# Latent attention and a squared-ReLU layer on one core: value product in 128x32 tiles with a turned result, batch 1's second scores by latents, batch 0's queries in two parts

## The chip, the cores and the metric

One core of one Trainium2 chip runs the whole kernel. The metric is the device time of one launch in microseconds (us), as the median of several runs. Engines: PE (matrix products; its weight loads are listed as PEld), DVE and ACT (elementwise work, copies out of PSUM), POOL (here it issues the loads) and SP (it issues most stores). PSUM has eight banks, numbered 0 to 7 here.

## The reference, cut to what matters

```python
batch, n_heads, seq, head_dim = (8, 8, 576, 64); n_pack = 32
n_tokens, d_model, d_ff = (4608, 512, 2048)

def sm_attn(qq, kk, vv):
    s = scale * np.matmul(qq, kk.transpose(0, 1, 3, 2))
    s = s - np.max(s, axis=-1, keepdims=True)
    a = np.exp(s)
    a = a / (np.sum(a, axis=-1, keepdims=True) + 1e-09)
    return np.matmul(a, vv)
p_packed = sm_attn(p, k, v)            # 32 latents for each head
out = sm_attn(q, p_packed, p_packed)   # 576 tokens look at 32 latents

x = out.transpose(0, 2, 1, 3).reshape(B * S, H * D)
h = x @ w_in
r = np.maximum(h, 0.0)
return (r * r) @ w_out
```

## The kernel before, in words

For each batch, eight heads are worked on as two "quads" (qd) of four. The steps of a batch have names that the plan uses:

- Tk, Tq: DVE turns keys and queries (32x32 blocks) so that the head dimension stands on partitions. `tr_q` turns all 576 positions of a quad at once.
- S1, SX, E: first scores of 32 latents against 576 keys, softmax over the keys, and five 128x128 transposes on PE for each quad, which put the keys on partitions (tile `e1`).
- PV (`pv`, L500 to 511): the value product. The values stand as weights, 128x64, and the softmax weights stream, 32 columns. For each of eight heads five matmuls add up, 40 in a batch. Two column tiles (e = 0, 1) stand beside each other. The result has the head dimension on partitions, which is what the steps behind it want. Quad 0's twenty may be issued before quad 1's softmax is ready.
- XT: `extract` copies that result to `ppT` (bf16), `spread` distributes it over partitions with four small matmuls, and four `pq_block` copies put it into a block-diagonal tile `pq_bd`.
- M (`m`): latents times `w_in`, so that the first layer later needs only the 32 weights a head instead of 64 dimensions. 16 matmuls in a burst, two bursts a batch, each taking a pair of banks and banks 4 and 5.
- S2: second scores. Batches 2 to 7 are in `TURNED`: the latents stand as weights (`s2_both`, L590, 32 matmuls on eight tiles of 64x32), and DVE turns the scores (`s2_turn`, L601) and later the softmax weights (`n_turn`, L609) with 32x32 block transposes. Batch 1 has tokens as weights: `s2` (L578, 16 matmuls), `s2_rest` (L665, 4), and later nine PE transposes (`s2_trh`, L724) with copies. Batch 0 (`SOLO`) does its scores in parts, SA.0.0, SA.0.1, SB.0.1 and SC.0.2, of which the first two need only the first 256 positions.
- C, N: softmax over 32 latents, and its result with latents on partitions (`a2`).
- F1: first layer, ReLU and square (for batch 0 in two parts: FA on 256 tokens, F1 on 320); 16 blocks of 128 features a batch. F2: second layer for each of 36 tiles of 128 tokens, 16 matmuls of 512 columns each, in the order of the feature blocks fb = 0 to 15; block fb needs pair fb // 2 of `w_out`, loaded as b0 to b7.

Nothing of the order is fixed by the source. A planner (`Plan`, L54 to 245) runs when the program is built: every step has pieces with an engine and a booked duration, what it depends on, which PSUM banks it takes and when it frees them; a list scheduler puts the ready piece of lowest priority number on its engine, and the instructions are issued in the order that comes out. A step's priority is a level plus a number from `TABLE` (L248 to 293). For a load it is -200 + 5 x (its place in `ORDER`) plus that number:

```python
ORDER = ("k0 v0 q0 i0 a0 a1 a2 a3 b0 b1 k1 b2 b3 v1 b4 b5 q1 b6 b7 p2 "
         + " ".join(f"k{b} v{b} q{b}" for b in range(2, B)))
```

Here a is `w_in`, b is `w_out`. The loads up to k2 are streams of their own, so their priorities alone set their order on POOL; those behind come in the order of the list. All are issued by POOL. In front of the output matmuls, where PE would be idle, the planner puts matmuls on zeros (`keep_clock`, L348), whose results nobody reads. Matmuls of different tile shapes belong to different modes, and the planner books 0.098 us for each change of mode (`TURN`).

Of the kernel before, what the change touches and what calls it, by code (L numbers as in the profile page):

```python
# [8 lines left out]
ACT = mybir.ActivationFunctionType  # L9
ALU = mybir.AluOpType  # L10
AX = mybir.AxisListType
F32 = mybir.dt.float32
# [41 lines left out]
class Plan:  # L54
# [193 lines left out]
TABLE = {'o': {'P.0': -451.53, 'X.0': -384.22, 'P.2': -273.87, 'X.1': -102.86, 'La0': -820.75, 'La1': -800.82,  # L248
# [45 lines left out]


def kernel_impl(tc, q, k, v, p, w_in, w_out, out):
    nc = tc.nc
    B, H, S, Dh = q.shape
    assert Dh == D and S == JT * 32 and H == 2 * QH
    NQD = H // QH  # L300
    DMODEL, DFF = w_in.shape
    NE = w_out.shape[1]
    NFB = DFF // FB
# [14 lines left out]
    with ExitStack() as ctx:  # L318
# [36 lines left out]
        def bank(u, j=0):  # L355
            return half(u[j])
# [827 lines left out]
```

## Time and profile before

| | us |
|---|---|
| median of 3 runs | 252.06 (251.58 to 252.1) |
| the profiled execution, time | 252.03 |
| the profiled execution, span | 250.3 |
| PE busy in the span | 239.2 |
| DVE busy | 185.2 |
| ACT busy | 165.7 |
| granted PE clock, mean | 0.999 |

Times in the views are counted from the start of the span. A timeline row gives start, duration, engine, line, operation, output and input tiles, form and count; in square brackets stands how long the engine was idle ahead of it and what ended that. A matmul's duration includes its way through the array, so what a burst costs PE is read from its first start to the first start behind it. Rows of groups give total busy time, then the mean in nanoseconds of one instruction. Rows of windows give the stretch, its length, and the busy time of PE, PEld, DVE, ACT and POOL with counts. Copies out of PSUM have the lines of a helper (L364 on ACT, L366 on DVE), so they are told apart by their tiles.

### The profile page before, as it was taken

How to read it: one execution, taken by the hardware profiler on the slowest of the kernel's cores; microseconds unless marked ns; L12 is line 12 of the kernel's file. 1: busy time of each engine (PE TensorE's matmuls, PEld its weight loads, DVE VectorE, ACT ScalarE, POOL GpSimd, SP SyncE). 2: the span in 40 equal slices, each digit the busy share in tenths (PEclk: the TensorE clock that was granted, in tenths of full speed). 3: DMA queues.
4: the chain of work that ended last, by engine and by line, in shares of the span. 5: the costliest groups of instructions: out<-in, count | busy, mean ns of one | idle time of the engine just before them, and what ended most of it. 6: DMA issues, size and time to landing. Idle time of an engine off the chain costs nothing.

```text
span 250.3 us, 5864 instructions
## 1 busy us (share of the span) xinstructions
PE 239.2 (96%) x2334; PEld 133.2 (53%) x2334; DVE 185.2 (74%) x356; ACT 165.7 (66%) x292; POOL 43.0 (17%) x76
## 2 busy tenths in 40 slices
PE   6788999999999999999999999999999999999992
PEld 4464465365544665466453564565435554466641
DVE  5779868794799999847698899646998667866100
ACT  8548799587638668699457688588066853587010
POOL 8845553423343310000000000000000000000000
PEclk9999999999999999999999999999999999999999
DMA  6999999999999999611111110310222102301222
GB/s 105 200 204 207 202 197 208 204 242 242 204 224 243 206 245 195 137 50 45 42 45 38 50 42 3 87 43 0 66 64 59 27 3 63 101 6 42 76 77 61
DMA packets 26715, 28.50 MB, mean 114 GB/s; under 512 B 5440, under 2 KB 18112, under 8 KB 26688
## 3 DMA queue, kind: packets, MB, share of 16 engines
q0 software_dynamic: 18960, 18.55, 45.2%
q1 hardware_dynamic: 6960, 9.32, 13.6%
q8 instruction: 18, 0.29, 0.4%
q10 hardware_dynamic: 768, 0.26, 0.4%
q14 instruction: 9, 0.07, 0.1%
HBM read 37.22 MB, written 9.44 MB: 186 GB/s over the span
## 4 chain that ended last, share of the span: by engine, by line
PE 80%; DMA 16%; issue 1%; POOL 1%; ACT 1%; DVE 0%; ACTq 0%; DVEq 0%; POOLq 0%
PE pb L806 46%; PE ps L750 22%; DMA w_out_b<-in_moe_w_out_dram 9%; DMA v_b<-in_v_dram 7%; PE ps L564 2%; PE pb L509 2%; PE ps L469 2%; PE pb L823 1%; PE pb L494 1%; PE pb L564 1%; PE ps L597 1%; PE pb L597 0%; POOL k_b L414 0%; ACT pq_bd L364 0%; PE pb L521 0%
## 5 line engine op out<-in xcount | busy, mean ns | idle before, releaser
L806 PE MATMUL pb<-w_out_b,gT 128*128 128x512 bf16 x560 | 144.0, 380 | 0.8 <-ACT gT L779 0.5
L806 PEld LDWEIGHTS <-gT 128*128 128x128 bf16 x560 | 51.8, 98 | 56.5 <-issue 6.0
L788 ACT ACTIVATE r<-ps 128x576 bf16<-128x576 f32 x112 | 71.0, 652 | 15.0 <-PE ps L750 11.6
L750 PE MATMUL ps<-a,M 128*128 128x288 bf16 x448 | 70.9, 286 | 0.0
L798 DVE TENSOR_TENSOR gT<-r 128x576 bf16<-128x576 bf16 x112 | 49.2, 453 | 26.3 <-ACT r L788 25.7
L750 PEld LDWEIGHTS <-M 128*128 128x128 bf16 x448 | 43.4, 98 | 22.3 <-issue 2.3
L364 ACT COPY o_sb<-pb 128x512 f32<-128x512 f32 (+1 forms) x17 | 9.6, 568 | 25.2 <-PE pb L806 21.2
L366 DVE COPY o_sb<-pb 128x512 f32<-128x512 f32 (+2 forms) x21 | 13.4, 641 | 14.7 <-PE pb L823 12.8
L481 ACT ACTIVATE e1x<-ps,n 128x576 bf16<-128x576 f32 x16 | 11.8, 738 | 13.1 <-DVE n L477 11.9
L364 ACT CAST M<-ps 128x1024 bf16<-128x1024 f32 (+1 forms) x15 | 14.7, 982 | 3.6 <-PE ps L564 3.6
L364 ACT CAST M<-pb 128x512 bf16<-128x512 f32 x28 | 15.5, 598 | 0.0
L709 ACT ACTIVATE e<-d 128x1152 bf16<-128x1152 f32 (+2 forms) x9 | 9.1, 1010 | 7.7 <-DVE d L704 7.6
L477 DVE TENSOR_REDUCE n<-ps 128x1 f32<-128x576 f32 x16 | 11.6, 749 | 3.2 <-PE ps L469 2.8
L419 POOL DMA_DIRECT2D v_b<-in_v_dram x16 | 11.2, 699 | 13.6 <-DMA k_b<-in_k_dram 4.6
L445 DVE STREAM_TRANSPOSE kT<-k_b 128x576 f32<-128x576 f32 x16 | 11.8, 756 | 2.0 <-DMA k_b<-in_k_dram 2.0
L414 POOL DMA_DIRECT2D q_b<-in_q_dram x16 | 8.9, 561 | 22.9 <-DVE kT L445 11.6
L442 DVE STREAM_TRANSPOSE qT<-q_b 128x576 f32<-128x576 f32 x16 | 11.8, 758 | 0.8 <-DMA q_b<-in_q_dram 0.7
L715 DVE TENSOR_REDUCE t<-e 128x36 f32<-128x1152 bf16 (+2 forms) x9 | 10.3, 1150 | 2.5 <-ACT e L709 2.4
L350 PE MATMUL pb<-zero 128*128 128x256 bf16 x64 | 10.4, 307 | 1.1 <-DVE zero L369 1.1
L364 ACT COPY e<-pb 128x640 bf16<-128x640 bf16 x14 | 9.5, 699 | 2.8 <-PE pb L494 2.8
L414 POOL DMA_DIRECT2D k_b<-in_k_dram x16 | 8.7, 544 | 13.9 <-DMA q_b<-in_q_dram 4.1
L721 DVE TENSOR_TENSOR n<-e,r 128x1152 bf16<-128x1152 bf16 (+2 forms) x9 | 10.4, 1157 | 0.2
(95 smaller groups left out, 232.9 us busy)
## 6 DMA issues: line engine op xcount, KB each, us to landing
out_dram<-o_sb SPq DMA_DIRECT2D x141, 64.0 KB, 1.7
k_b<-in_k_dram POOLq DMA_DIRECT2D x16, 288.0 KB, 12.0
q_b<-in_q_dram POOLq DMA_DIRECT2D x16, 288.0 KB, 12.0
v_b<-in_v_dram POOLq DMA_DIRECT2D x8, 320.0 KB, 12.2
v_b<-in_v_dram POOLq DMA_DIRECT2D x8, 256.0 KB, 11.8
w_in_b<-in_moe_w_in_dram POOLq DMA_DIRECT2D x8, 256.0 KB, 10.1
w_out_b<-in_moe_w_out_dram POOLq DMA_DIRECT2D x8, 256.0 KB, 10.6
p_b<-in_p_dram POOLq DMA_DIRECT2D x1, 192.0 KB, 10.6
```

What stands on the lines that cost most here:

```text
L364: nc.scalar.copy(dst, src)
L366: eng.tensor_copy(dst, src)
L414: nc.gpsimd.dma_start(t, src[self.b, qd * QH:(qd + 1) * QH].rearrange("h (a j) d -> (h a) (j d)", j=JT))
L419: nc.gpsimd.dma_start(self.v[64 * i:64 * i + 64, :, :n * D], src[:, :, i * GM * D:(i * GM + n) * D])
L442: nc.vector.transpose(self.qT[:, qd].rearrange("p s x -> p (s x)").bitcast(F32), self.t.q[qd][:].bitcast(F32))
L445: nc.vector.transpose(kT[:, qd].rearrange("p s x -> p (s x)").bitcast(F32).rearrange("p (x a j2) -> p j2 x a", a=32, j2=2), self.t.k[qd][: ...
L477: nc.vector.tensor_reduce(self.n1[:, qd:qd + 1], self.ps1[qd], axis=AX.X, op=ALU.max, negate=True)
L481: nc.scalar.activation(e1x[:, qd], self.ps1[qd], ACT.Exp, bias=self.n1[:, qd:qd + 1], accum_out=self.d1[:, qd:qd + 1])
L750: nc.tensor.matmul(ps[:, c], lhsT=a.M[:, qd, fb * FB:(fb + 1) * FB], rhs=a.a2[:, qd, c * HALF:(c + 1) * HALF], start=(qd == 0), stop=(qd = ...
L788: nc.scalar.activation(dst, src, ACT.Relu)
L798: eng.tensor_tensor(out=Att.cols(gT[:, fb, o:o + S]), in0=r, in1=r, op=ALU.mult)
L806: nc.tensor.matmul(po[t], lhsT=gT[:, fb, n0:n0 + P], rhs=w_out_b[:, fb, :], start=(fb == 0), stop=(fb == NFB - 1))
```

## The change

Four edits, and new numbers in `TABLE`.

1. In batches 1 to 7 the value product has its operands swapped: 128x32 slices of the softmax weights stand, values stream with 64 columns, and four heads' results stand beside each other in four column tiles. The result has latents on partitions, so it is cast to bf16 (`pp_out`), turned by one 128x128 transpose on PE (`pp_turn`), and extracted from there. It is one step, issued once both quads' softmax weights are ready. The first products M and the freeing of the bank wait for the later stages.
2. `TURNED` includes batch 1.
3. The queries of batch 0 are turned in two parts of 256 and 320 positions; SA waits for the first part, SB and SC for both.
4. The first scores of the next batch wait for the one product step.

```diff
-    TURNED = range(2, 8)
+    TURNED = range(1, 8)
...
+            def tr_qx(self, qd, a, z):
+                self.tile_of("qT", att, [P, NQD, S, 2], BF16, bufs=1)
+                nc.vector.transpose(self.qT[:, qd, a:z].rearrange("p s x -> p (s x)").bitcast(F32), self.t.q[qd][:, 2 * a:2 * z].bitcast(F32))
...
+            def pv_both(self, u):
+                self.ps_bank = bank(u)
+                self.ps_pp = self.ps_bank[:, :P]
+                for e in range(2):
+                    for g in range(GM + 1):
+                        for x in range(2 * NQD):
+                            qd, h = x // 2, x % 2 * 2 + e
+                            c0 = self.at(qd, h) * NP
+                            nc.tensor.matmul(self.ps_pp[32 * x:32 * x + 32, 64 * e:64 * e + 64], lhsT=self.e1[:, qd, g, c0:c0 + NP],
+                                             rhs=self.t.v[:, qd * QH + h, g * D:(g + 1) * D], start=(g == 0), stop=(g == GM))
+            def pp_out(self, eng):
+                self.tile_of("ppn", small, [P, P], BF16, bufs=1)
+                cast(eng, self.ppn, self.ps_pp)
+            def pp_turn(self):
+                self.ps_t = self.ps_bank.bitcast(BF16)[:, 2 * P:3 * P]
+                nc.tensor.transpose(self.ps_t, self.ppn[:], ident[:])
...
-                cast(eng, self.ppT[:].rearrange("p qd pr i -> p (qd pr i)"), self.ps_pp)
+                cast(eng, self.ppT[:].rearrange("p qd pr i -> p (qd pr i)"), self.ps_t)
...
+            if b == 0 and nm == "q":
+                return [Step(f"Tq.0.{qd}", [[[("DVE", 0.36, lambda qd=qd: T[0].tr_qx(qd, 0, 2 * P))]]], [f"Lq.0.{qd}"]) for qd in QDS] + [
+                        Step(f"TR.0.{qd}", [[[("DVE", 0.43, lambda qd=qd: T[0].tr_qx(qd, 2 * P, S))]]], [f"Tq.0.{qd}"], (), [("kqb", 0, f"Lq.0.{qd}")]) for qd in QDS]
...
-            after = [f"X.{min(b // 2, 1)}"] + ([f"PV.{b - 1}.{qd}" for qd in QDS] if b else []) + gate(b, 1)
+            after = [f"X.{min(b // 2, 1)}"] + ([f"PV.{b - 1}.{qd}" for qd in QDS if b == 1 or qd == 0] if b else []) + gate(b, 1)
...
-            return [Step(nm, [[[("PE", 0.33, lambda: T[b].pv(0, U[nm]))]]],
-                         [f"E.{b}.0", f"Lv.{b}.0", f"Lv.{b}.1", "I2" if b else "I"], banks=AB, mode=1),
-                    Step(f"PV.{b}.1", [[[("PE", 0.33, lambda: T[b].pv(1, U[nm]))]]],
-                         [f"E.{b}.1"], (), [("vb", 0, f"Lv.{b}.0")], mode=1),
-                    Step(f"XT.{b}", [[[("-", 0.0, lambda: None)]],
-                                     [[("DVE", 0.21, lambda: T[b].extract(V)),
-                                       ("ACT", 0.17, lambda: T[b].extract(A))]],
+            return [Step(nm, [[[("PE", 0.41, lambda: T[b].pv_both(U[nm]))]]],
+                         [f"E.{b}.{qd}" for qd in QDS] + [f"Lv.{b}.0", f"Lv.{b}.1", "I2"], (), [("vb", 0, f"Lv.{b}.0")], banks=AB, mode=3),
+                    Step(f"XT.{b}", [NO, [[("DVE", 0.21, lambda: T[b].pp_out(V)), ("ACT", 0.19, lambda: T[b].pp_out(A))]],
+                                     [[("PE", 0.06, lambda: T[b].pp_turn())]],
+                                     [[("DVE", 0.21, lambda: T[b].extract(V)), ("ACT", 0.19, lambda: T[b].extract(A))]],
                                      [[("PE", 0.115, lambda: T[b].spread())]],
...
-                return [Step(f"M.{b}.{c}", [[[("PE", 0.48, lambda c=c: mm(c))]], outs(c)], [f"XT.{b}/1.0"] + pre(c),
+                return [Step(f"M.{b}.{c}", [[[("PE", 0.48, lambda c=c: mm(c))]], outs(c)], [f"XT.{b}/3.0"] + pre(c),
```

`TABLE` is replaced as a whole, 'o' (priorities), 'l' (leanings of ACT) and 'w', 'm'. Of its numbers the prediction speaks of these:

```diff
-    'La0': -820.75, 'La1': -800.82, 'La2': -637.86, 'La3': -641.44, 'Lb0': -695.2, 'Lb1': -707.23, 'Lk1': -677.21, 'Lb2': -517.0,
-    'Lb3': -374.76, 'Lv1': -640.82, 'Lb4': -338.41, 'Lb5': -313.97, 'Lq1': -513.07, 'Lb6': -267.76, 'Lb7': -214.55, 'Lp2': -521.7, 'Lk2': -193.36
+    'La0': -1045.51, 'La1': -646.79, 'La2': -569.12, 'La3': -571.27, 'Lb0': -635.25, 'Lb1': -462.5, 'Lk1': -628.7, 'Lb2': -848.69,
+    'Lb3': -521.4, 'Lv1': -541.33, 'Lb4': -368.14, 'Lb5': -247.48, 'Lq1': -489.49, 'Lb6': -232.97, 'Lb7': -147.19, 'Lp2': -464.73, 'Lk2': -223.43
```

More of the change, by code (lines that the diff above doesn't have):

```diff
@@ L245, in use @@
         self.wait, self.margin = z.get("w", 0.0), z.get("m", 0.0)
-TABLE = {'o': {'P.0': -451.53, 'X.0': -384.22, 'P.2': -273.87, 'X.1': -102.86, 'La0': -820.75, 'La1': -800.82,
[45 rows of a table removed]
+TABLE = {'o': {'P.0': -17.44, 'X.0': -515.84, 'P.2': -467.13, 'X.1': -217.88, 'La0': -1045.51, 'La1': -646.79,
[47 rows of a table added]
 def kernel_impl(tc, q, k, v, p, w_in, w_out, out):
@@ L514, in extract @@
                 self.tile_of("ppT", small, [P, NQD, 2, NP], BF16)
-                cast(eng, self.ppT[:].rearrange("p qd pr i -> p (qd pr i)"), self.ps_pp)
+                cast(eng, self.ppT[:].rearrange("p qd pr i -> p (qd pr i)"), self.ps_t)
             def spread(self):
-                self.ps_pq = self.ps_bank[:, P:2 * P]
+                self.ps_pq = self.ps_bank[:, 2 * P:3 * P]
                 for x in range(2):
@@ L931, in pv_steps @@
                                        ("ACT", 0.21, lambda h=h: T[b].pq_block(h, A))] for h in range(QH)]],
-                         [f"PV.{b}.1"], free=[(3, nm)])]
+                         [nm], free=[(5, nm)])]
         def m_steps(b):
@@ L965, in m_steps @@
                     Step(f"MX.{b}.0", [NO, outs(0)], [f"M.{b}.0"], free=[(1, f"M.{b}.0")]),
-                    Step(f"M.{b}.2", [[[("PE", 0.48, lambda: mm(2))]], outs(2)], [f"XT.{b}/1.0"] + pre(2),
+                    Step(f"M.{b}.2", [[[("PE", 0.48, lambda: mm(2))]], outs(2)], [f"XT.{b}/3.0"] + pre(2),
                          banks=[x + (4, 5) for x in HB], free=[(1, None)], mode=2)]
@@ L973, in s2_steps @@
         def s2_steps(b):
-            pre = ([f"XT.{b}.{qd}" for qd in QDS] if b in SOLO else [f"XT.{b}"]) + [f"Tq.{b}.{qd}" for qd in QDS] + ([f"N.{b - 1}.{qd}" for qd in QDS] if b else [])
+            pre = ([f"XT.{b}.{qd}" for qd in QDS] if b in SOLO else [f"XT.{b}"]) + [f"T{'q' if b else 'R'}.{b}.{qd}" for qd in QDS] + ([f"N.{b - 1}.{qd}" for qd in QDS] if b else [])
             nm = f"S2.{b}.0"
@@ L1084, in kernel_impl @@
         setup()
-        plan.levels.update(L=-99, I=-99, LP=-99, I2=5, P=-9, X=-8, G=0, T=0, S1=1, SX=1, E=1, PV=1, XT=1, S2=2, SA=2, SB=2.5, SC=2.6, C=2, N=2, M=3, MX=3, SR=2, FA=14, F1=15, F2=30)
+        plan.levels.update(L=-99, I=-99, LP=-99, I2=5, P=-9, X=-8, G=0, T=0, S1=1, SX=1, E=1, PV=1, XT=1, S2=2, SA=2, SB=2.5, SC=2.6, TR=2.3, C=2, N=2, M=3, MX=3, SR=2, FA=14, F1=15, F2=30)
         plan.stream([Step("P.0", [[[("DVE", 0.2, lambda: nc.vector.tensor_copy(p_b[:, :2 * NQD], p_f))]],
```

92 rows, old and new, of the table TABLE are left out of this document.

## The prediction

> **What bounds the kernel now.** I read the page first, for the span and the chain that ended last (80% of it PE), and then busy time by windows: one row of the front, the sum of the steady stretch, and the sum over the first 50 us of line L350 alone.
>
> ```profile
> span 250.3 us, 5864 instructions
> ...
> PE 80%; DMA 16%; issue 1%; POOL 1%; ACT 1%; DVE 0%; ACTq 0%; DVEq 0%; POOLq 0%
> ...
> 24.00:26.00 2.00, 2.00 (x18) 1.30 (x17) 2.00 (x5) 1.94 (x4) 0.63 (x2) 1.00 1.24 205
> ...
> sum 194.00, PE 193.31 PEld 106.14 DVE 144.74 ACT 127.33 POOL 14.25; mean PE 48.33 PEld 26.53 DVE 36.19 ACT 31.83 POOL 3.56
> ...
> sum 50.00, PE 10.36 PEld 6.44; mean PE 0.55 PEld 0.34
> ```
>
> PE is the bound. The first sum covers 52 to 246 us, after the front, in four windows: PE is busy 193.31 of 194.00 us, DVE 144.74, ACT 127.33. So after 52 us a microsecond less work on PE is a microsecond less time, as long as PE finds other matmuls to issue, and DVE and ACT have about a quarter to spare. L350 are the filler matmuls that keep the clock up, 10.36 us of them, all issued while the first batches still come in. Behind them, up to 52 us, PE is also nearly full: from 24 to 26 us it is busy 2.00 of 2.00, DVE 2.00 and ACT 1.94. But there what it may issue depends on loads, so a saving in the front counts only if the front as a whole moves up. The profiled execution took 252.03 us, 1.73 us more than its span; the median of three is 252.06, so a sum made against the one holds for the other.
>
> **The value product, batches 1 to 7.** Rows from the timeline: batch 4 (one burst), batch 2 (the only one issued in two bursts), the transposes of batch 3, a plain run of output matmuls from the chain.
>
> ```profile
> 118.81 2.32 PE L806 MATMUL pb<-w_out_b,gT 128*128 128x512 bf16 x10
> 121.07 0.81 PE L509 MATMUL pb<-e,v_b 128*64 128x32 bf16 x40
> 121.81 0.39 PE L806 MATMUL pb<-w_out_b,gT 128*128 128x512 bf16 x1
> ...
> 62.15 0.49 PE L509 MATMUL pb<-e,v_b 128*64 128x32 bf16 x20
> 62.57 0.66 PE L750 MATMUL ps<-a,M 128*128 128x288 bf16 x4
> ...
> 69.07 0.49 PE L509 MATMUL pb<-e,v_b 128*64 128x32 bf16 x20
> 69.49 0.70 PE L469 MATMUL ps<-kT,pT_bd 64*32 64x512 bf16 x32
> ...
> 80.74 0.72 PE L494 MATMUL pb<-ident,e1n 128*128 128x128 bf16 x10
> 81.30 1.03 PE L806 MATMUL pb<-w_out_b,gT 128*128 128x512 bf16 x4
> ...
> 229.79 5.18 PE pb L806 x24
> ```
>
> A plain output matmul takes 5.18/24 = 0.216 us of PE. Ten from 118.81 fill PE until 120.97, so the change of tile shape ahead of the product costs 0.10 us, and the 40 matmuls hold PE until 121.81, 0.74 us. A batch in one burst costs 0.84; batch 2, in two bursts of 0.42 with a change ahead of each, 1.04. Removed: 6 x 0.84 + 1.04 = 6.08 us.
>
> Added: 40 matmuls of 64 columns, with 32-column weights, in four column tiles. The trace has no such form. An upper bound is the old burst, 0.74: twice the columns, but no fewer instructions. A lower bound comes from the second scores, which use four column tiles already:
>
> ```profile
> 125.07 0.29 PE L597 MATMUL ps<-qT,pq_bd 64*32 64x288 bf16 x1
> ...
> 125.50 0.29 PE L597 MATMUL ps<-qT,pq_bd 64*32 64x288 bf16 x1
> 125.71 2.33 PE L806 MATMUL pb<-w_out_b,gT 128*128 128x512 bf16 x10
> ```
>
> Thirty-two matmuls of 288 columns on eight tiles hold PE for 0.64 us. In the timeline they start in four waves 0.125 us apart, which is 2.3 columns a nanosecond, and what is left, 0.64 - 0.50 = 0.14, is the drain behind the last. Forty times 64 columns over four tiles are 640 columns: 640/2.3 = 0.28, with the drain 0.42. I take 0.48, near the lower end, because this row has four column tiles standing beside each other as the new form has, and the old burst only two. The transpose added between the two casts is one 128x128 matmul, 0.56/10 = 0.056 us. A batch then costs 0.10 + 0.48 + 0.06 = 0.64. Batches 2 to 7: 5 x 0.20 + 0.40 = 1.40 us saved (bounds: 1.76 saved, 0.16 lost); batch 1: 0.20 saved (0.26 saved, 0.06 lost).
>
> A rule speaks against this: the Trainium skill, TensorE: Matmul & The Clock Gate, section "Wait — 56ns, not 53.3ns?", has it that matmuls never start closer than about 25 ns however few their columns. By it 40 cost at least 1.0 us in either form and nothing is saved here. The trace doesn't keep it: the old burst has 0.74/40 = 18.5 ns a matmul, the second scores (125.50 - 125.07)/31 = 13.9 ns.
>
> What hangs on the longer way from product to blocks: cast, transpose and cast instead of one cast. The added cast is off PE; at seven of them DVE and ACT have room by the sums above. PE issues in order, so behind the transpose the next output matmuls would wait for the cast; the plan books it behind other ready matmuls, as it does now with the spread behind its cast. I cost it at nothing; uncovered it would be about 0.3 us a batch, 2 us in all. The bank is held longer by the same hop, which matters only to the next product, many microseconds later.
>
> **Second scores of batch 1.**
>
> ```profile
> 38.41 1.06 PE L584 MATMUL ps<-pq_bd,qT 128*128 128x128 bf16 x16
> 39.40 0.30 PE L678 MATMUL pb<-pq_bd,qT 128*64 128x128 bf16 x4
> 39.63 0.72 PE L763 MATMUL ps<-a,M 128*128 128x320 bf16 x4
> ...
> 50.47 0.61 PE L730 MATMUL pb<-ident,n 128*128 128x128 bf16 x8
> 50.97 1.67 PE L806 MATMUL pb<-w_out_b,gT 128*128 128x512 bf16 x7
> 52.48 1.14 PE L750 MATMUL ps<-a,M 128*128 128x288 bf16 x8
> ...
> 44.88 1.35 DVE L715 TENSOR_REDUCE t<-e 128x36 f32<-128x1152 bf16 x1 [2.15 <-ACT e L709]
> ...
> L605 DVE STREAM_TRANSPOSE d<-ps 128x576 f32<-128x576 f32 x6 | 4.7, 779 | 1.1 <-PE ps L597 1.0
> L607 DVE STREAM_TRANSPOSE d<-pb 128x288 f32<-128x288 f32 x12 | 4.8, 441 | 0.0
> L613 DVE STREAM_TRANSPOSE a<-n 128x576 bf16<-128x576 bf16 x10 | 7.3, 757 | 0.1
> ...
> 135.38 1.44 DVE L613 STREAM_TRANSPOSE a<-n 128x576 bf16<-128x576 bf16 x2
> ```
>
> Removed from PE: 39.63 - 38.41 = 1.22 for the scores and 50.97 - 50.47 = 0.50 for nine transposes. Added: the latents' form, 0.10 + 0.64 = 0.74. Saved: 0.98 us. DVE gets the turns, 0.78 + 2 x 0.44 + 2 x 0.76 = 3.2 us, and loses two copies from PSUM; maximum and difference stay. It idles for 2.15 us ahead of 44.88 waiting for ACT, and that covers most of it; uncovered, it is 2 us on the start of F1.1. The chain also gets shorter: before, 52.48 - 38.41 = 14.1 us from scores to F1.1; batch 4, which has the new form, took 136.82 - 125.07 = 11.75.
>
> **Queries of batch 0 in parts.**
>
> ```profile
> L395 DVE STREAM_TRANSPOSE pT<-p_b 128x384 f32<-128x384 f32 x1 | 0.6, 568 | 0.0
> L395 DVE STREAM_TRANSPOSE pT<-p_b 128x128 f32<-128x128 f32 x1 | 0.3, 311 | 0.0
> ...
> 13.24 1.72 ACT L364 CAST pq_bd<-pb 32x64 bf16<-32x64 f32 x8 [0.66 <-PE pb L543]
> 14.14 0.38 PE L630 MATMUL pb<-pq_bd,qT 128*128 128x128 bf16 x4 [0.36 <-ACT pq_bd L364]
> ```
>
> Linear between the two rows, a part of 256 is 0.44 and one of 320 is 0.50, against 0.76 for 576 columns (L613 above): 0.18 more DVE for each quad, but its first half comes 0.32 earlier. PE waits here for ACT, which does all eight blocks; a freer DVE can take some. I take 0.2 us earlier for everything behind (bounds: 0.15 later, 0.6 earlier). It is filler time that goes.
>
> **The order of the loads.** The new numbers of TABLE move loads on POOL's queue. A load's priority is -200 + 5 times its place in ORDER + its number: w_out pair 1 goes from -862 to -618, pair 2 from -662 to -994, pair 7 from -325 to -257, batch 2's keys from -293 to -323. Lowest first, that gives a0, b2, a1, b0, k1, a2, a3, v1, b3, b1, q1, p2, b4, b5, b6, k2, b7, where it was a0, a1, b1, b0, k1, a2, a3, v1, b2, q1, p2, b3 to b7, k2.
>
> ```profile
> 23.34 0.71 POOL L426 DMA_DIRECT2D w_out_b<-in_moe_w_out_dram  x1 [0.72 <-DMA k_b<-in_k_dram]
> 24.75 0.58 POOL L414 DMA_DIRECT2D q_b<-in_q_dram  x1 [0.70 <-DMA k_b<-in_k_dram]
> 36.98 0.54 POOL L414 DMA_DIRECT2D k_b<-in_k_dram  x1 [0.88 <-DMA q_b<-in_q_dram]
> ...
> w_out_b<-in_moe_w_out_dram POOLq DMA_DIRECT2D x8, 256.0 KB, 10.6
> ...
> 23.46 0.82 PE L806 MATMUL pb<-w_out_b,gT 128*128 128x512 bf16 x3 [0.47 <-ACT gT L779]
> ...
> 31.76 0.60 PE L806 MATMUL pb<-w_out_b,gT 128*128 128x512 bf16 x2
> ...
> 44.10 2.75 PE L806 MATMUL pb<-w_out_b,gT 128*128 128x512 bf16 x12 [0.30 <-DMA w_out_b<-in_moe_w_out_dram]
> ```
>
> Pair 1 takes the place of the first q1 load, 24.75, and lands 10.6 later, at 35.4; the queries of batch 1 slip one place, 1.4 us. Pair 7 takes the second k2 place, 36.98, and lands at 47.6, where PE now waited for it until 44.10. The output tiles add in order of pairs, so with pair 1 missing each open tile stops after two matmuls. Before, twelve ran from 23.46 to 31.76, all ahead of pair 2's landing at 33.9, so on pairs 0 and 1: three tiles of four. Now three tiles have two each: six fewer, 6 x 0.216 = 1.3 us that PE can't fill then. Bounds: none lost, if first-layer work fills it, and 1.3 plus the 3.5 us by which pair 7 is late. I take 1.3, because between 44.1 and 47.6 the first products of batch 1 and a third tile can run, while between 24 and 32 nothing else is ready. F1.1 starts no earlier than its queries allow: 39.8 + 11.75 = 51.55, 0.9 before 52.48, so the front's 0.98 + 0.20 + 0.2 saved less 1.3 lost is not held up by it.
>
> **Sum.** -1.40 in the steady stretch, -1.18 in the front, -0.2 at the start, +1.3 from the late pair 1: -1.48. 252.03 - 1.48 = 250.55, so 250.5 us. Its own range is 249.7 to 251.4.
>
> **Rivals.** (1) *All of it comes*: first-layer work fills the hole of pair 1; 252.03 - 2.78 = 249.2. For it: between 24 and 36 there is first-layer work left that only DVE and ACT hold back. Against: those two are full there, by the row of 24 to 26 us. (2) *The new form is no faster*: 0.74 a burst whatever the tiles; the steady stretch loses 0.16, batch 1 0.06, and 252.03 + 0.16 + 0.06 - 0.98 - 0.2 + 1.3 = 252.4, no change. For it: weights change with each matmul in both forms. Against: the 13.9 ns of the second scores, whose weights change as well. The 25 ns of the Trainium skill's page TensorE: Matmul & The Clock Gate would end here too. (3) *The loads decide*: pair 7 at 47.6 stops all open output tiles, because batch 1's scores and products now claim banks 4 and 5 together with a pair and leave fewer tiles open; PE idles up to 3.5 us more, 250.55 + 3.5 = 254.0. It is slower once more than 2.0 of the 3.5 stay unfilled, 252.55. For it: PE waits for this very load at 44.10 today. Against: M.1 and a third tile (eight matmuls, 1.7 us) are there to fill most of it.
>
> **Chances.** The forecast 0.46, (1) 0.19, (2) 0.14, (3) 0.21. A measurement of this kernel tells about 0.2%, 0.5 us, from no change. Faster by more: the forecast and (1), 0.65; within: (2), 0.14; slower: (3), 0.21. The range reaches from 248.9, a little beyond (1) for the lower bound of the new burst, to 253.0, the first half of (3).
>
> **What would show it.** Right: bursts of the new product of 0.4 to 0.55 us from first start to the next instruction; a change of shape of 0.10 ahead; no wait of PE for the cast ahead of the turn; nine transposes fewer around 50 us; four to eight output matmuls before 35 us where there were twelve; filler ending up to 0.5 us sooner; F1.1's first matmul near 51.5. Wrong: bursts of 0.74 (the 0.48 fails); PE idle for a microsecond or more on w_out_b after 44 us (rival 3); twelve output matmuls before 35 us (the 1.3 fails); PE waiting for DVE in batches 2 to 7, which would say that the steady stretch is no longer PE's alone.

## The result, and the profile after

| | before | after |
|---|---|---|
| median, us | 252.0 (251.58 to 252.1, 4 runs) | 250.56 (250.5 to 250.9, 4 runs) |
| profiled execution, us | 252.03 | 250.5 |
| its span, us | 250.3 | 248.7 |

The ratio of after to before is 0.9949, with a 95% interval of 0.9931 to 0.9966: 1.3 us faster, give or take 0.45. The forecast was 250.5. In the profiled executions the span is 1.6 us shorter.

First the page of the changed kernel (the span, and the share of each engine in the chain that ended last), then its busy time in the window of 52 to 246 us, all of one stretch, with the columns length, PE, PEld, DVE, ACT and POOL.

```profile
span 248.7 us, 5896 instructions
...
PE 77%; DMA 16%; POOL 2%; ACT 1%; issue 1%; DVE 0%; DVEq 0%; ACTq 0%; POOLq 0%
```

```profile
sum 194.00, PE 191.81 PEld 104.56 DVE 144.54 ACT 128.23 POOL 14.27; mean PE 191.81 PEld 104.56 DVE 144.54 ACT 128.23 POOL 14.27
```

PE is still what sets the end. Its sum fell from 193.31 to 191.81 only because its last matmuls end 1.5 us sooner, at 243.90 us instead of 245.41, both within the window (first before, then after):

```profile
244.35 1.06 PE L823 MATMUL pb<-w_out_b,gT 128*128 128x128 bf16 x16
242.84 1.06 PE L848 MATMUL pb<-w_out_b,gT 128*128 128x128 bf16 x16
```

Ahead of its last matmul PE idles for 0.1 us of the window in both. DVE and ACT carry what they carried, although DVE or ACT now makes one more cast a batch.

The changed lines themselves: the timeline of PE around the product of batch 4 (start, duration), and the groups of the product and of the turn (total busy, mean of one in ns, idle time ahead).

```profile
110.06 0.81 PE L831 MATMUL pb<-w_out_b,gT 128*128 128x512 bf16 x3
110.80 0.49 PE L514 MATMUL pb<-v_b,e 128*32 128x64 bf16 x40
111.22 1.19 PE L775 MATMUL ps<-a,M 128*128 128x288 bf16 x8
112.25 0.22 PE L523 MATMUL pb<-ident,ppn 128*128 128x128 bf16 x1
112.30 0.59 PE L831 MATMUL pb<-w_out_b,gT 128*128 128x512 bf16 x2
```

```profile
L514 PE MATMUL pb<-v_b,e 128*32 128x64 bf16 x280 | 3.4, 195 | 0.0
L523 PE MATMUL pb<-ident,ppn 128*128 128x128 bf16 x7 | 1.5, 219 | 0.0
```

Three output matmuls of 0.216 us fill PE from 110.06 to 110.71; the burst starts at 110.80, and PE goes on at 111.22. So the change of shape costs 0.09 and the burst 0.42 us, in all seven batches, where it was 0.74. The turn costs 0.05, and no idle time stands ahead of it: the longer way through a cast is covered everywhere.

The start times of the single matmuls in the trace show how the 0.42 comes about. In batch 4 they start in groups of four, one for each column tile, and most groups follow 29 ns apart; the last one starts at 0.29 us, and the next instruction comes 0.13 later. Before, they started in pairs, one for each of two column tiles, 31 to 32 ns apart, so that the last one started only at 0.63.

What happened in the front is read from windows of the first 54 us, first before, then after. The first window that is shown holds batch 0's start, the second is where the late w_out pair was to be felt, the third goes on to the end of the loads. Below the rows for all instructions stand, for after, those of the filler line L352 alone; before, the filler was 10.36 us, all of it in the first 22 us.

```profile
0.00:22.00 22.00, 16.94 (x179) 11.38 (x180) 16.11 (x41) 13.78 (x33) 14.62 (x31) 1.00 1.07 176
22.00:28.00 6.00, 5.38 (x40) 2.92 (x39) 5.33 (x11) 5.36 (x11) 3.13 (x5) 1.00 1.20 203
28.00:50.00 22.00, 21.53 (x225) 11.61 (x224) 17.06 (x33) 18.15 (x29) 10.46 (x17) 1.00 1.31 203
50.00:54.00 4.00, 4.00 (x37) 2.70 (x36) 3.93 (x11) 2.87 (x7) 1.07 (x2) 1.00 1.12 252
```

```profile
0.00:22.00 22.00, 17.77 (x180) 11.95 (x180) 15.93 (x43) 13.28 (x32) 14.42 (x30) 1.00 1.06 173
22.00:28.00 6.00, 4.70 (x39) 2.57 (x35) 5.09 (x11) 5.32 (x12) 2.75 (x6) 1.00 1.20 204
28.00:50.00 22.00, 21.32 (x230) 10.63 (x227) 19.71 (x34) 21.07 (x35) 10.86 (x17) 1.00 1.32 202
50.00:54.00 4.00, 4.00 (x50) 1.85 (x49) 3.61 (x7) 2.02 (x6) 1.14 (x3) 1.00 1.11 220
```

```profile
0.00:22.00 22.00, 11.02 (x66) 6.87 (x66) 1.00 1.06 173
22.00:28.00 6.00, 0.83 (x6) 0.51 (x6) 1.00 1.20 204
```

Work of PE without filler, window by window: 6.58, 5.38, 21.53 and 4.00 before; 17.77 - 11.02 = 6.75, 4.70 - 0.83 = 3.87, 21.32 and 4.00 after. By 54 us the changed kernel has done 1.55 us less, nearly all of it missing between 22 and 28 us. The second scores and the product of batch 1, which lie in this time, need 0.98 + 0.27 us less of PE than before. So at 54 us the changed kernel is behind by 1.55 - 1.25 = 0.3 us. This is read from one execution of each: batch 0's first keys, whose load the change doesn't move, were turned at 6.05 us before and at 5.74 after, and in the experiments at 5.5 to 6.9, so a few tenths may be scatter. Behind it, six products give back 5 x 0.275 + 0.475 = 1.85 (0.84, and 1.04 for batch 2, less 0.09 + 0.42 + 0.055). The difference is 1.55, against 1.6 in the spans.

### The profile page after: what moved, and what is told of

Same layout as the page of the kernel before. It is cut to its first block, busy times and chain, and to the rows that moved or that the text cites. A ratio compares the mean times of both kernels' runs of the same rounds, so it can differ in the third digit from the quotient of the medians.

```text
span 248.7 us, 5896 instructions
## 1 busy us (share of the span) xinstructions
PE 237.6 (96%) x2352; PEld 130.5 (52%) x2352; DVE 186.9 (75%) x356; ACT 168.3 (68%) x302; POOL 42.9 (17%) x76
## 4 chain that ended last, share of the span: by engine, by line
PE 77%; DMA 16%; POOL 2%; ACT 1%; issue 1%; DVE 0%; DVEq 0%; ACTq 0%; POOLq 0%
PE pb L831 45%; PE ps L775 22%; DMA w_in_b<-in_moe_w_in_dram 8%; DMA w_out_b<-in_moe_w_out_dram 4%; DMA q_b<-in_q_dram 4%; PE ps L589 2%; PE ps L475 2%; PE pb L848 1%; PE pb L500 1%; PE ps L622 1%; PE pb L589 1%; PE pb L514 1%; ACT r L813 1%; POOL k_b L416 0%; POOL q_b L416 0%
## 5 line engine op out<-in xcount | busy, mean ns | idle before, releaser
L831 PE MATMUL pb<-w_out_b,gT 128*128 128x512 bf16 x544 | 138.2, 380 | 0.7 <-DMA w_out_b<-in_moe_w_out_dram 0.6
L823 DVE TENSOR_TENSOR gT<-r 128x576 bf16<-128x576 bf16 x112 | 49.7, 455 | 26.5 <-ACT r L813 25.4
L775 PEld LDWEIGHTS <-M 128*128 128x128 bf16 x448 | 42.9, 98 | 20.5 <-issue 1.3
L366 ACT COPY o_sb<-pb 128x512 f32<-128x512 f32 (+1 forms) x18 | 10.3, 571 | 23.8 <-PE pb L831 19.8
L368 DVE COPY o_sb<-pb 128x512 f32<-128x512 f32 (+2 forms) x19 | 12.1, 638 | 14.5 <-PE pb L848 12.8
L366 ACT CAST M<-pb 128x512 bf16<-128x512 f32 x30 | 16.5, 600 | 1.3 <-PE pb L589 1.3
L352 PE MATMUL pb<-zero 128*128 128x256 bf16 x72 | 11.9, 317 | 1.1 <-DVE zero L371 1.1
L444 DVE STREAM_TRANSPOSE qT<-q_b 128x576 f32<-128x576 f32 x14 | 10.3, 755 | 0.4 <-DMA q_b<-in_q_dram 0.4
```

Source lines behind the costliest of these rows:

```text
L352: nc.tensor.matmul(half(7)[:, :2 * P], lhsT=zero[:, :P], rhs=zero, start=True, stop=True)
L366: nc.scalar.copy(dst, src)
L368: eng.tensor_copy(dst, src)
L775: nc.tensor.matmul(ps[:, c], lhsT=a.M[:, qd, fb * FB:(fb + 1) * FB], rhs=a.a2[:, qd, c * HALF:(c + 1) * HALF], start=(qd == 0), stop=(qd = ...
L823: eng.tensor_tensor(out=Att.cols(gT[:, fb, o:o + S]), in0=r, in1=r, op=ALU.mult)
L831: nc.tensor.matmul(po[t], lhsT=gT[:, fb, n0:n0 + P], rhs=w_out_b[:, fb, :], start=(fb == 0), stop=(fb == NFB - 1))
```

## Experiments

Ratios are to the kernel before on the same chip. Each diff is against the changed kernel, where nothing else is said. The changed kernel was not run again beside the experiments, so a few tenths between its 250.56 us and theirs can't be told from nothing.

### The old product in the new order

```diff
             def pv_both(self, u):
-                for e in range(2):
...
+                for qd in range(NQD):
+                    self.pv(qd, None)
...
             def pp_turn(self):
-                self.ps_t = self.ps_bank.bitcast(BF16)[:, 2 * P:3 * P]
-                nc.tensor.transpose(self.ps_t, self.ppn[:], ident[:])
+                self.ps_t = self.ps_pp
```

> The changed kernel with the product of before (128x64 tiles, no turn, no cast ahead of it) in batches 1 to 7, all instructions of all engines in the same order otherwise. If the product's time on PE is time of the kernel: bursts go from 0.42 back to 0.74 us, seven transposes of 0.056 go, 7 x 0.26 = +1.8 us, 252.4 us. If the gain of the steady stretch came from the order that the plan found anew and not from the product: within 0.5 us of 250.6.

252.11 us (251.66 to 253.87), ratio 1.0003 [0.9987, 1.0019]; the span is again 250.3. The timeline of PE at the same place as above:

```profile
110.54 0.81 PE L824 MATMUL pb<-w_out_b,gT 128*128 128x512 bf16 x3
111.28 0.81 PE L527 MATMUL pb<-e,v_b 128*64 128x32 bf16 x40
112.02 1.16 PE L768 MATMUL ps<-a,M 128*128 128x288 bf16 x8
```

0.74 is back, and with it the whole gain. Seven times 0.32, less seven turns of 0.05, and 0.23 more in batch 3, whose burst takes 0.97 here, make 2.1; PE's wait for pair 7 is 0.42 shorter (0.21 instead of 0.63), which leaves the 1.6 or so of the spans. Everything else in the change, its order included, adds up to nothing within about 0.4 us: what one part saves another loses.

### The product issued twice

Batches 2 to 7 issue the product's 40 matmuls twice; the second pass overwrites the first with the same values.

```diff
-                for e in range(2):
+                for e in [0, 1] * (2 if self.b > 1 else 1):
```

> The changed kernel with the product of batches 2 to 7 issued twice over (the second pass overwrites the first with the same values). If a microsecond of PE in the steady stretch is a microsecond of time: 40 more matmuls at 0.28 to 0.42 us for each of six batches, +1.7 to +2.5 us, 252.3 to 253.1 us. If PE has slack there that the busy sum doesn't show (rival): less than half of that, under 251.4 us.

252.50 us, ratio 1.0007 [0.9987, 1.0027], span 251.2, 2.5 more than the changed kernel's.

```profile
111.24 0.81 PE L831 MATMUL pb<-w_out_b,gT 128*128 128x512 bf16 x3
111.98 0.82 PE L514 MATMUL pb<-v_b,e 128*32 128x64 bf16 x80
112.74 1.15 PE L775 MATMUL ps<-a,M 128*128 128x288 bf16 x8
```

Eighty hold PE for 0.76, forty for 0.42: 0.34 for forty more, 8.4 ns each. From the last start to the next instruction it is 0.13 us in both. Six times 0.34 is 2.0, and in batch 3 the burst took 0.22 more (0.98); together 2.25 of the 2.5. Most of the rest is PE's wait for pair 7, which is 0.96 in this execution instead of 0.63. A microsecond of PE behind the front is a microsecond of time, in this direction as in the other.

### One column tile after the other

```diff
-                    for g in range(GM + 1):
-                        for x in range(2 * NQD):
+                    for x in range(2 * NQD):
+                        for g in range(GM + 1):
```

> The changed kernel with the loops of the product swapped: the five matmuls of one head one after the other in the same column tile, then the next tile. Same instructions, same order of everything else. If four column tiles working side by side make the short burst: a matmul then waits for the one before it in its tile, 25 to 40 ns each, bursts of 1.0 to 1.6 us, +4 to +8 us, 254.7 to 258.8 us. If the rate at which PE issues small matmuls sets it (10.5 ns each): bursts stay 0.42 and the time 250.6 us.

251.15 us, ratio 0.9968 [0.9955, 0.9981], span 249.5.

```profile
111.03 0.63 PE L514 MATMUL pb<-v_b,e 128*32 128x64 bf16 x40
111.60 1.15 PE L775 MATMUL ps<-a,M 128*128 128x288 bf16 x8
```

The burst is 0.57, so both expectations miss. Issuing five matmuls in a row into one tile costs 0.15 a burst, 7 x 0.15 = 1.0 where the span shows 0.8. Most of the gain from narrow tiles (0.74 to 0.57) doesn't come from neighbours in the queue going to different tiles. The single matmuls suggest why. Eight of the forty have a longer duration (0.20 instead of 0.19 us), and they start at 0, 45, 89, 135, 179, 223, 268 and 318 ns. If these are the first of each head's five, which the trace doesn't name, the starts between them fit five matmuls of a head about 30 ns apart, as in the other order, and a next tile that begins 44 to 50 ns after the one before instead of behind all of its five: the tiles still work side by side.

### Batch 0's queries whole again

The order is kept; the first of the two turns does all 576 positions, the second nothing.

```diff
-... lambda qd=qd: T[0].tr_qx(qd, 0, 2 * P)
+... lambda qd=qd: T[0].tr_q(qd)
-... lambda qd=qd: T[0].tr_qx(qd, 2 * P, S)
+... lambda: None
```

> The changed kernel with batch 0's queries turned whole at the place of their first part; same order otherwise. If the parts bring what the prediction took: the first block of the first layer starts 0.2 to 0.5 us later and the time is 250.8 to 251.1 us. If the path to the first layer runs through another wait (the blocks on ACT, the loads): no change, 250.4 to 250.7 us.

250.23 us (249.72 to 250.63), ratio 0.9929 [0.9914, 0.9944], which overlaps that of the changed kernel. Its first block of the first layer starts at 20.69 us, in the changed kernel at 20.73, and in the kernels of the first three experiments, which have the changed kernel's front, at 21.06 to 21.49. So the parts bring nothing that these runs can show.

### Batch 1's second scores by tokens again

```diff
-    TURNED = range(1, 8)
+    TURNED = range(2, 8)
```

The plan is made anew.

> The changed kernel with batch 1's second scores as before the change (tokens as weights, PE transposes of the softmax weights); plan made again, steady stretch almost the same. By the prediction's price of that edit PE gets 0.98 us more work in the front: 251.5 us. If the front is not PE's (waits for loads and DVE in it have room for 1 us): within 0.4 us of 250.5. If the shorter way from scores to the first layer counts as well: more than 1.3 us, over 251.8 us.

251.56 us, ratio 0.9956 [0.9932, 0.9979], span 250.1. On the same chip the kernel of the next experiment, whose span differs from the changed one's by 0.1, had 250.40. The 0.98 us of PE that the latents' form saves agree with these medians, which lie 1.2 apart; all ten runs of this kernel (from 250.92) are above all six of the other (to 250.90). By the ratio alone it would not differ from the changed kernel. The 1.4 us in the spans is no price: 0.93 of it stands there already where the second part of batch 0's first layer begins (28.13 instead of 27.20), ahead of batch 1's second scores, and the granted clock of this execution was 0.72 from 6 to 12 us.

### Pair 1 of the output weights early

```diff
-    'Lb1': -462.5, ... 'Lb2': -848.69,
+    'Lb1': -838.69, ... 'Lb2': -472.5,
```

Pairs 1 and 2 change places in the loads; the new plan moves only four output matmuls forward.

> The changed kernel with pairs 1 and 2 of w_out in each other's place in the order of the loads; the plan made again, which moves four output matmuls ahead of 30 us and leaves the rest nearly as it is. If the late pair 1 is what empties PE between 24 and 28 us: four matmuls of 0.216 fill that hole, -0.9 us, 249.7 us. If the front ends by something later, pair 7 at 48 us or batch 1's softmax (rival): the hole closes and the wait ahead of pair 7 grows by as much, within 0.3 us of 250.5.

250.40 us (250.32 to 250.9), ratio 0.9909 [0.9878, 0.9939], span 248.6: no change in the spans. The windows of this kernel, and PE's wait behind them:

```profile
22.00:28.00 6.00, 5.98 (x45) 3.14 (x42) 5.86 (x13) 6.00 (x13) 3.08 (x5) 1.00 1.21 204
28.00:50.00 22.00, 19.89 (x221) 10.15 (x220) 19.11 (x33) 20.85 (x34) 10.48 (x16) 1.00 1.32 203
```

```profile
48.27 0.59 PE L831 MATMUL pb<-w_out_b,gT 128*128 128x512 bf16 x2 [1.80 <-DMA w_out_b<-in_moe_w_out_dram]
```

The hole of 22 to 28 us is closed but for the filler (0.83), and 1.80 us stand ahead of 48.27 instead, where pair 7 lands. Up to 54 us there are 64 output matmuls to issue, here as before and after; the ones issued early are missing later.

### Pair 7 ahead of batch 2's keys

```diff
-    'Lb7': -147.19,
+    'Lb7': -230,
```

> The changed kernel with pair 7 of w_out loaded ahead of batch 2's keys, as before the change; plan made again. If the wait of 0.6 us on pair 7 at 48 us counts: it goes, -0.6 us, 249.9 us. If batch 2's first scores, whose keys now come later, or F1 of batch 1 hold the front anyway: 250.3 to 251 us.

252.73 us, ratio 1.0011 [0.9986, 1.0036], span 251.3; both expectations miss. The wait for pair 7 is gone, but the keys come later, batch 2's first scores stand at 51.28 instead of 50.69, and behind them the stock of output matmuls is used up:

```profile
51.92 2.12 PE L831 MATMUL pb<-w_out_b,gT 128*128 128x512 bf16 x9
55.54 0.93 PE L500 MATMUL pb<-ident,e1n 128*128 128x128 bf16 x10 [1.50 <-DVE e1n L494]
```

With these plans, batch 2's keys ahead of pair 7 are worth more than the wait that they cause.

### The kernel before with the loads of after

Against the kernel before: its 17 numbers for the loads up to k2 are replaced by those of after, and the plan is made anew.

> The kernel before with the changed numbers for the loads up to k2, nothing else; plan made again. If the new order of loads costs what the prediction took: +1.3 us, 253.3 us, with fewer than nine output matmuls ahead of 35 us. If it costs nothing because other work fills PE: 251.7 to 252.3 us.

259.37 us, ratio 1.0276 [1.0228, 1.0323]. The waits of PE (total, times, longest):

```profile
PE ps L564 <- ACT e1x L481: 2.7, 1, 2.7
...
PE ps L750 <- ACT M L364: 1.0, 1, 1.0
```

I had expected 1.3 us; it is 6.8, against 252.58 for the kernel before on the same chip. The plan that came out put batch 1's second burst of M behind batch 2's first scores, and the two waits there are 3.7 of it; the rest was not traced to a cause. So this run prices a plan, and not the order of the loads by itself.

### Without batch 2's keys

Neither the load nor the turn of batch 2's keys is issued, and batch 2 computes with the keys of batch 1. The order of everything else stays, once that of the changed kernel, once that with pair 1 early.

```diff
-... lambda nm=nm, qd=qd: L[b].dma_kq(nm, qd)
+... lambda nm=nm, qd=qd: None if (b, nm) == (2, "k") else L[b].dma_kq(nm, qd)
-... (T[b].tr_k if nm == "k" else T[b].tr_q)(qd)
+... None if (b, nm) == (2, "k") else (T[b].tr_k if nm == "k" else T[b].tr_q)(qd)
```

> The changed kernel with the same order on every engine, but batch 2's keys are neither loaded nor turned (batch 2 computes its first scores with the keys of batch 1). On POOL's queue everything behind them, output-weight pair 7 first, lands up to 2 x 1.4 us earlier. Theory: two shortages make the front of the changed kernel 1.7 us longer in filler and idle PE time; from 22 to 28 us (0.83 filler and 1.30 idle, against 0.61 before) because pair 1 isn't there, and at 48.2 us (0.63) because pair 7 isn't. Then the wait at 48.2 us goes and the holes from 22 to 28 us stay: 250.56 - 0.6, 249.8 to 250.1. Rival: the front's length is set by batch 1's way from its queries to its first layer, whatever is loaded; the 0.6 us turn up as another idle stretch before 54 us, and the time is 250.4 to 250.7.

250.29 us (250.07 to 251.5), ratio 0.9931 [0.991, 0.9951]: 0.3 below 250.56, between the two expectations, and within the interval of no change.

> The same with pairs 1 and 2 exchanged in the loads, so that both shortages are taken away: the kernel with pair 1 early waited 2.0 us for pair 7 instead of in 22 to 28 us. Theory: that wait goes, PE is full from 21 us on, and the time is 250.40 - 2.0, 248.4 to 248.9, which is the 1.5 to 1.8 us that the load order cost. Rival (batch 1's own way decides): output matmuls run out earlier and PE idles before the first layer of batch 1 instead: 250.1 to 250.6.

250.24 us (250.22 to 250.34), ratio 0.9923 [0.9901, 0.9946]: the rival's time. The same two windows:

```profile
22.00:28.00 6.00, 5.91 (x49) 3.30 (x47) 5.85 (x13) 5.88 (x13) 3.13 (x5) 1.00 1.20 204
28.00:50.00 22.00, 20.40 (x224) 10.45 (x227) 17.98 (x33) 21.19 (x35) 10.30 (x17) 1.00 1.32 203
```

Of 1.80 us at pair 7 only 0.49 are left, at 44.47, but 0.85 us stand at 49.38, where an output matmul waits for a bank that ACT still empties. One thing blurs this trace: batch 0's first keys were turned at 6.71 us, in the changed kernel at 5.74, and by 22 us PE had done 0.5 us less. The edit doesn't touch these keys, and other kernels that don't touch them either have them at up to 6.86, so this is scatter between executions; the granted clock, 0.72 from 6 to 12 us here, may add to it. The four runs agree within 0.12 us, so the time doesn't hang on this one execution.

### Batch 0's second part ahead of batch 1's keys

The timelines of DVE, before and after, suggest another reason for the hole from 22 to 28 us: with the new plan batch 0's second part loses its place.

```profile
19.29 0.68 DVE L704 TENSOR_TENSOR d<-pb,m 128x512 f32<-128x512 f32 x1
...
22.34 0.68 DVE L715 TENSOR_REDUCE t<-e 128x16 f32<-128x512 bf16 x1
```

```profile
22.19 0.69 DVE L729 TENSOR_TENSOR d<-pb,m 128x512 f32<-128x512 f32 x1
23.68 0.78 DVE L451 STREAM_TRANSPOSE kT<-k_b 128x576 f32<-128x576 f32 x1 [0.80 <-DMA k_b<-in_k_dram]
24.38 0.64 DVE L740 TENSOR_REDUCE t<-e 128x16 f32<-128x512 bf16 x1
```

The subtraction comes 2.9 us later, then DVE stands 0.80 us for batch 1's keys, and the sum that was at 22.34 is at 24.38. PE's first block of the second part follows at 27.20, where it was at 25.35. The experiment issues these steps in their old places:

```diff
-        for p in sorted(out, key=lambda p: p.start):
+        early = {("SB.0.1", 2): 19.71, ("SB.0.1", 3): 20.36, ("SB.0.1", 4): 21.47, ("SB.0.1", 5): 21.48,
+                 ("N.0.1", 0): 24.395, ("N.0.1", 1): 24.396, ("S1.1.0", 0): 24.84, ("F1.0.0", 0): 24.9}
+        for p in sorted(out, key=lambda p: early.get((p.step.name, p.stage), p.start)):
```

> The changed kernel, with eight steps issued earlier or later in the same plan: on DVE and ACT the softmax of batch 0's second part (subtraction, exponent, sum, scaling) stands ahead of the softmax of its last 64 positions and ahead of the turn of batch 1's keys, where before had it; its transposes and its first block of the first layer stand ahead of batch 1's first scores on PE. Reason: in the changed kernel DVE subtracts at 22.19 us (before 19.29), then stands 0.80 us for batch 1's keys, and PE reaches the second part of the first layer at 27.20 us (before 25.35). Theory 1 (the order on DVE is the whole of the 1.7 us): first block of the second part at 25.5 to 26.0 us, idle and filler time of 22 to 28 us down from 2.1 to 1.0 us or less, and the time down by as much: 249.2 to 249.7. Theory 2 (pair 7 lands at 48.2 us whatever is done earlier, and there is a fixed stock of output matmuls until then): the hole closes as well, the wait for pair 7 grows from 0.63 to 1.5 to 2.0 us, and the time stays, 250.2 to 250.6.

250.79 us (250.09 to 250.95), ratio 0.9947 [0.9934, 0.996]: no change. Its window of 22 to 28 us, of which 0.83 us of PE are filler, and PE's timeline:

```profile
22.00:28.00 6.00, 5.00 (x41) 2.91 (x41) 4.95 (x11) 4.74 (x11) 3.19 (x5) 1.00 1.20 204
...
25.95 0.70 PE L790 MATMUL ps<-a,M 128*128 128x320 bf16 x4
...
27.83 0.61 PE L462 MATMUL ps<-kT,pT_bd 128*128 128x512 bf16 x2 [0.84 <-ACT e1x L489]
```

The block starts at 25.95, as expected, and 0.84 us of waiting for ACT appear at 27.83 in its place. So the hole is not closed: idle and filler are 1.83 us, where theory 1 asked for 1.0 or less and theory 2 for a closed hole, and the changed kernel has 2.13, and PE's work without filler is 4.17 instead of 3.87. The order on DVE is thus not the whole of it, which theory 1 said; what a closed hole is worth, this run can't tell. Theory 2 has the time, but not its reason, since the wait for pair 7 is 0.2 us here and not 1.5.

> The same order in the kernel without batch 2's keys and with pairs 1 and 2 exchanged, which took 250.24. Theory 2: with the late load gone as well, the closed hole counts: 249.0 to 249.5. Rival (from 24 to 50 us ACT and DVE are full, 21.2 of 22 us for ACT behind 28 us, and PE waits for banks that ACT has to empty): no change, 250.0 to 250.4, and PE idles on ACT between 44 and 50 us for 1 us or more.

250.61 us (250.09 to 253.16), ratio 0.996 [0.9932, 0.9989]: theory 2 falls, the rival's 250.0 to 250.4 is missed by 0.2 within its spread. The window and the wait:

```profile
28.00:50.00 22.00, 20.41 (x225) 10.44 (x222) 17.92 (x34) 21.54 (x36) 10.41 (x17) 1.00 1.32 203
```

```profile
PE pb L833 <- ACT M L368: 0.8, 1, 0.8
PE pb L833 <- DMA w_out_b<-in_moe_w_out_dram: 0.5, 1, 0.5
```

Here the hole is closed but for 1.0 us of idle and filler. PE idles for 1.6 us between 28 and 50 us while ACT is busy for 21.54 of 22; of that, 0.8 is waiting for ACT in one place, where the rival asked for 1 or more.

## Why the prediction was right

**What bounds it** was right. Behind the front the engines do what they did, PE is busy throughout, and both directions were tried: the old product costs 1.6 us of span, a second copy 2.5.

**The product** was right in its mechanism, and the saving was put too small by a quarter. Taken at 0.48, measured 0.42, the lower bound that the second scores gave, and in both of its parts: 0.29 to the last start and 0.13 behind it, for 0.28 and 0.14; the change of shape 0.09 for 0.10, the turn 0.05 for 0.056. The saving in batches 2 to 7 is 1.85 instead of 1.40. The row to hold to was the nearest in kind, the one with four column tiles, and I moved away from it by 0.06 without a row that asked for it. The rival of an unchanged 0.74 fell with the burst itself, and with it the rule of the Trainium skill, TensorE: Matmul & The Clock Gate, section "Wait — 56ns, not 53.3ns?", that starts don't come closer than about 25 ns, if it is taken for PE as a whole: here they come 7.5 ns apart on average. Within one column tile the trace agrees with it, at 29 ns.

**No wait ahead of the turn** was right: no idle time is listed for it, in any batch.

**Second scores of batch 1** were right: 0.72 us for the new burst (0.09 and 0.63, from 40.20 to 40.92), 0.74 forecast, and 1.2 us between medians when it is undone, 0.98 forecast.

```profile
39.98 0.38 PE L831 MATMUL pb<-w_out_b,gT 128*128 128x512 bf16 x1
40.29 0.30 PE L622 MATMUL ps<-qT,pq_bd 64*32 64x288 bf16 x1
...
40.92 0.82 PE L831 MATMUL pb<-w_out_b,gT 128*128 128x512 bf16 x3
```

**Queries in parts** were wrong. The first layer did start 0.24 us sooner (20.73 for 20.97), but the kernel without the parts does so as well (20.69), and three kernels with them start it at 21.06 to 21.49, so the 0.24 is scatter between executions. The step that failed is the claim that a sooner first half moves everything behind it; no run shows it to move anything.

**The late pair 1** was right in place, size and cause, and wrong in its price. The forecast was 1.3 us that PE can't fill between 24 and 35 us, with four to eight output matmuls before 35; there are four, and 1.5 us are missing from 22 to 28. With pair 1 early 1.3 of them come back (5.98 less 0.83 of filler, for 3.87), with batch 0's old order on DVE only 0.3. But with pair 1 early the hole moves to 48 us and the time stays. The step that failed is the one that took a hole for a loss: between 22 and 54 us PE has a fixed amount to do, and it is held again at the next thing that is late.

**F1.1's first matmul** came at 53.71, not near 51.5, which is 13.4 us behind the scores at 40.29 and not 11.75. The queries weren't what held it: DVE and ACT order it behind batch 1's M casts and batch 2's row maxima. It cost nothing, because PE is full from 48.22 us on; as a gauge of the front it was badly chosen, since the changed kernel has both M bursts of batch 1 ahead of it and the kernel before only one.

**The filler** didn't end sooner but later, at 22.7 us instead of 20.7 (six of 72 matmuls stand at 22.03).

**The rivals.** That everything comes (249.2) didn't happen: the front gave back what it saved. That pair 7 stops PE didn't either: it lands at 48.2 and costs 0.63 us.

So the sum of 1.48 was met by 1.55 with two terms off: 0.45 more from the product, 0.4 less from the front, which was forecast to gain 0.08 and lost 0.3. That the two nearly cancel is luck.

**What stays open** is what holds the front. Five kernels that move work or loads there, three of them with loads taken away, stayed within 0.35 us of the changed one, and where a hole closed another opened; a sixth, with pair 7 ahead of batch 2's keys, lost 2.2. The engine that is nearly full from 28 to 50 us is ACT: 21.07 of 22 us in the changed kernel, 20.85 with pair 1 early, 21.19 without batch 2's keys as well, 21.54 in the last one, but 18.15 before, where batch 1's second M burst with its casts came only behind 54 us. That speaks for ACT; a kernel with less for ACT to do in this time was not tried.

## What to carry to other kernels

In a stretch where one engine is busy throughout, price a change by the time between the first start of a burst and the next instruction, and take it from the row that is nearest in tiles; here that was right to 0.01 us. In a stretch where loads and three engines are all nearly late, a hole is no loss by itself: ask what would stop the same engine next if the hole were filled, and count work done by the end of the stretch rather than idle time. And when a remade plan comes with a change, run the change in the new order without its parts, as what looks like an effect of an edit may be the order's, or the scatter of a single execution.

## What the runs showed of the hardware that was not expected

Matmuls of 64 columns into four column tiles of 128x32 start 7.5 ns apart on average (0.29 us from the first of forty to the last; 8.4 ns for each of forty more), half of the 16 ns of 32 columns into two tiles of 128x64 (0.63 us), although they carry twice the columns. A single column tile takes its next matmul after 29 ns in the one form and after 31 to 32 in the other, so what counted was the number of tiles and not the columns. And five matmuls in a row into the same tile, each adding to the one before, cost only 0.15 us over forty, 3.7 ns each, compared with going round the four tiles. The Trainium skill, TensorEngine Tiling (Array Packing), section "Instruction Overhead", puts about 60 cycles of overhead on each matmul, so that a short one takes as long as one of 60 columns. Within a tile the trace agrees, since 32 columns took no less than 64; across tiles the cost is shared, since both orders of issue start a matmul every 7.5 or 11 ns on average.
